# Zero fills of two large gradients: from an SBUF tile, or copied from DRAM to DRAM in 16 KB pieces

## The chip, the cores and the metric

The kernel runs on one core of a Trainium2 chip; the core that shares its memory is idle. The metric is the device time of one execution in microseconds (us). A ratio is the mean time of one kernel's fast runs over the mean of the other's fast runs of the same rounds, so it is not quite the ratio of the medians that are quoted.

## The reference, cut to what matters

The reference is the forward and backward pass of one decoding token through a modulated layer norm, a sliding-window attention over cached keys and values, and a gated MLP (FFN). For the change only the gradients of the caches matter:

```python
Hq, Hkv, Sk, Dh = (32, 4, 65536, 128)
W = min(4096, max(256, Sk // 4))                       # window: the last 4096 rows
k = jnp.repeat(k_cache[:, :, Sk - W:, :], rep, axis=1)
v = jnp.repeat(v_cache[:, :, Sk - W:, :], rep, axis=1)
...
_out, _vjp = jax.vjp(_f, A_x, A_k_cache, A_v_cache, A_wq, A_wo, B_w_gate, ...)
```

Outputs 2 and 3 are the gradients of the two caches, 4 x 65536 x 128 in bf16 each. Only the last 4096 rows of each head are not zero. The other 61440 rows are 15 MiB of zeros per head, and 8 heads in the two tensors make 120 MiB (125.8 MB) of zeros to write.

## The kernel before: the parts that matter

The zeros are written in 120 fills of 1 MiB from one zeroed tile. They are spread over the program by lists of counts (`Z_MOD`, `Z_FFN` and so on), so that they fill whatever time the other transfers leave. In the FFN loop ScalarE's queue issues them; elsewhere GpSimd's queue does.

```python
ZW = 4096
zeros = vt([P, ZW], "zeros", BF16)                     # 128 partitions x 8 KB
nc.vector.memset(zeros.bitcast(U32), 0)
...
for og in (out_2, out_3):
    for g in range(G):
        region = og[0, g, 0:SKW, :].rearrange("r d -> (r d)").rearrange("(p x) -> p x", p=P)
        for i in range(region.shape[1] // ZW):
            zregions.append(region[:, i * ZW:(i + 1) * ZW])
zleft = list(zregions)

def zero(n, after=None, q=None):
    for _ in range(n):
        if not zleft:
            return
        ins = (q or nc.gpsimd).dma_start(out=zleft.pop(0), in_=zeros[:, :])
        if after is not None:
            dep(ins, after)                            # wait for a step of the program: pacing
```

One round of the FFN loop (seven in all), cut to its transfers:

```python
zero(Z_FFN[5 * n], None, nc.scalar)
...
nc.sync.dma_start(out=wd_dram(out_8, n), in_=wd_t[n])
if n + 1 < NB:
    load_wg(n + 1)                                     # GpSimd queue, as load_wu
for j in range(KD):
    ...                                                # VectorE reads wu, ScalarE overwrites it
    if j % 4 == 3:
        zero(Z_FFN[5 * n + 1 + j // 4], None, nc.scalar)
nc.gpsimd.dma_start(out=dwu_view[:, :, n * FB:(n + 1) * FB], in_=wu)
...                                                    # the same for wg, two more places for fills
nc.gpsimd.dma_start(out=dwg_view[:, :, n * FB:(n + 1) * FB], in_=wg)
if n + 2 < NB:
    load_wu(n + 2)                                     # into a buffer that a store must leave first
```

## Time and profile before

| | before |
|---|---|
| time, median of 3 | 653.28 us (651.76 to 654.0) |
| bytes moved by the DMA engines | 262.63 MB, 404 GB/s on average |
| of these zero fills | 125.8 MB, 120 issues |
| memory traffic | 76.55 MB read, 185.60 MB written |
| busiest compute engine | VectorE, 49% of the span |

The row of DMA shares, the queues, the issues and the waits are shown in the prediction.

### The profile page before, as it was taken

Reading aid. Unit: us, or ns where it says so; the run is one execution under the profiler, and the core shown is the slowest. Engines: PE = TensorE matmul, PEld = TensorE weight load, DVE = VectorE, ACT = ScalarE, POOL = GpSimd, SP = SyncE. Lnnn points to the kernel's source line nnn. Section 1 sums busy time; section 2 is a strip of 40 time slices with the busy share of each in tenths; the row PEclk is TensorE's granted clock in tenths of the full one; section 3 lists DMA queues with packets and bytes.
Section 4 is the critical chain, followed back from the end, with each engine's and each line's share of the span. In section 5 each row is a group of like instructions: output and inputs, shape, how many; then the busy total and the mean of one; then the engine's idle time right before and its main releaser. Section 6 shows DMA issues by size and latency. Waiting matters only on the chain.

```text
span 650.8 us, 7106 instructions
## 1 busy us (share of the span) xinstructions
PE 149.7 (23%) x2784; PEld 127.4 (20%) x2784; DVE 319.7 (49%) x626; ACT 206.9 (32%) x306; POOL 83.0 (13%) x137
## 2 busy tenths in 40 slices
PE   3123227572201020010101101310670000424300
PEld 2123215572201020010101101300450000313200
DVE  3442005602737246081460814899700089996293
ACT  2000016611521613243133432789570000424800
POOL 2000000131010200102011010212111012112220
PEclk9999999865555555555555555575765555555555
DMA  8999999999999999999999999999999999999996
GB/s 335 430 428 422 426 426 413 404 418 397 421 425 415 416 417 393 414 388 408 417 356 419 361 409 415 392 382 412 388 415 422 415 425 426 425 407 388 410 411 251
DMA packets 43810, 262.63 MB, mean 404 GB/s; under 512 B 4096, under 2 KB 4096, under 8 KB 18432
## 3 DMA queue, kind: packets, MB, share of 16 engines
q0 software_dynamic: 23184, 131.08, 49.8%
q1 hardware_dynamic: 12048, 69.22, 26.0%
q10 hardware_dynamic: 8544, 61.88, 23.6%
q8 instruction: 22, 0.36, 0.2%
q14 instruction: 12, 0.10, 0.0%
HBM read 76.55 MB, written 185.60 MB: 403 GB/s over the span
## 4 chain that ended last, share of the span: by engine, by line
DMA 64%; DVE 14%; ACT 11%; PE 6%; issue 4%; POOL 0%; SPq 0%; POOLq 0%; ACTq 0%; DVEq 0%
DMA out_dram<-arena 28%; DMA arena<-in_B_w_gate_dram 18%; DMA arena<-in_w_mod_dram 7%; DVE arena L168 6%; DMA arena<-in_A_wq_dram 6%; ACT arena L172 5%; DMA arena<-in_A_k_cache_dram 5%; DVE junk L168 3%; PE tp_kv L342 2%; DVE arena L164 1%; ACT arena L345 1%; PE gu_ps L476 1%; ACT arena L230 1%; ACT du_b L508 1%; DMA out_dram<-dx_orow 1%
## 5 line engine op out<-in xcount | busy, mean ns | idle before, releaser
L168 DVE CUSTOM_DVE_ANT_0 arena<-arena 128x4096 bf16<-128x4096 bf16 (+1 forms) x24 | 80.1, 3350 | 51.4 <-DMA arena<-in_w_mod_dram 51.4
L476 PE MATMUL gu_ps<-h_bf,arena 128*128 128x1 bf16 x448 | 16.9, 172 | 192.1 <-DMA arena<-in_B_w_up_dram 103.5
L151 DVE TENSOR_TENSOR hh<-sg,gu_ps 128x4 f32<-128x4 f32 x7 | 1.1, 158 | 119.4 <-ACT om L481 119.4
L136 POOL DMA_DIRECT2D out_dram<-zeros x61 | 33.6, 554 | 185.0 <-PE q_ps L311 49.8
L476 PEld LDWEIGHTS <-arena 128*128 128x128 bf16 x448 | 16.2, 118 | 193.9 <-issue 166.7
L172 ACT ACTIVATE arena<-du_b,h 128x512 bf16<-128x512 bf16 x56 | 35.3, 710 | 36.0 <-DMA arena<-in_B_w_down_dram 32.3
L649 PEld LDWEIGHTS <-arena 8*128 8x128 bf16 x256 | 24.9, 127 | 106.1 <-issue 102.7
L172 ACT ACTIVATE arena<-dg_b,h 128x512 bf16<-128x512 bf16 x56 | 35.3, 708 | 26.4 <-issue 14.4
L345 ACT COPY arena<-tp_kv 128x1024 bf16<-128x1024 bf16 x13 | 13.1, 1010 | 89.7 <-PE tp_kv L342 89.7
L653 ACT CAST arena<-ps_kv 128x512 bf16<-128x512 f32 x32 | 16.1, 691 | 77.2 <-DMA out_dram<-arena 77.2
L168 DVE CUSTOM_DVE_ANT_0 junk<-arena,b1k 128x1024 bf16<-128x1024 bf16 x28 | 34.2, 1222 | 8.6 <-DMA arena<-in_B_w_down_dram 8.1
L168 DVE CUSTOM_DVE_ANT_0 arena<-arena,b1k 128x1024 bf16<-128x1024 bf16 x32 | 36.7, 1221 | 0.4 <-ACT b1k L230 0.4
L168 DVE CUSTOM_DVE_ANT_0 arena<-arena,du_b 128x512 bf16<-128x512 bf16 x56 | 34.8, 686 | 3.5 <-ACT du_b L508 3.5
L168 DVE CUSTOM_DVE_ANT_0 arena<-arena,dg_b 128x512 bf16<-128x512 bf16 x56 | 34.8, 685 | 0.0
L172 ACT ACTIVATE arena<-b1k,o_col 128x1024 bf16<-128x1024 bf16 x32 | 33.4, 1142 | 0.0
L649 PE MATMUL ps_kv<-DO_hd,arena 8*128 8x128 bf16 x128 | 15.3, 280 | 77.9 <-ACT arena L653 77.2
L342 PE MATMUL tp_kv<-ident_bf,arena 128*128 128x128 bf16 x256 | 22.1, 252 | 20.7 <-DMA arena<-in_A_k_cache_dram 13.0
L160 DVE COPY arena<-tp_kv 128x1024 bf16<-128x1024 bf16 x19 | 13.0, 690 | 28.1 <-PE tp_kv L342 28.1
L480 ACT ACTIVATE sg<-gu_ps 128x4 f32<-128x4 f32 x7 | 1.2, 174 | 76.3 <-PE gu_ps L476 76.3
L342 PEld LDWEIGHTS <-arena 128*128 128x128 bf16 x256 | 19.2, 115 | 23.6 <-DMA arena<-in_A_k_cache_dram 13.9
L429 POOL DMA_DIRECT2D arena<-in_B_w_up_dram x7 | 6.2, 890 | 134.4 <-DMA out_dram<-arena 134.4
L655 ACT ACTIVATE arena<-ps_kv 128x512 bf16<-128x512 f32 x32 | 16.1, 624 | 21.8 <-DMA out_dram<-arena 21.8
(185 smaller groups left out, 377.3 us busy)
## 6 DMA issues: line engine op xcount, KB each, us to landing
out_dram<-zeros POOLq DMA_DIRECT2D x61, 1024.0 KB, 20.4
out_dram<-zeros ACTq DMA_DIRECT2D x59, 1024.0 KB, 20.9
out_dram<-arena POOLq DMA_DIRECT2D x46, 1024.0 KB, 20.8
arena<-in_A_wq_dram SPq DMA_DIRECT2D x16, 1024.0 KB, 21.1
arena<-in_w_mod_dram SPq DMA_DIRECT2D x8, 1536.0 KB, 29.9
arena<-in_A_wo_dram SPq DMA_DIRECT2D x8, 1024.0 KB, 22.2
arena<-in_w_mod_dram SPq DMA_DIRECT2D x8, 1024.0 KB, 23.9
arena<-in_B_w_down_dram SPq DMA_DIRECT2D x7, 1024.0 KB, 11.9
```

Source lines behind the costliest of these rows:

```text
L136: ins = (q or nc.gpsimd).dma_start(out=zleft.pop(0), in_=zeros[:, :])
L160: return nc.vector.tensor_copy(out=out, in_=a)
L164: return nc.vector.tensor_scalar(out=out, in0=a, scalar1=s1, scalar2=None, op0=op0)
L168: return nc.vector.tensor_tensor_reduce(out=out, in0=w, in1=b, scale=1.0, scalar=0.0, op0=ALU.mult, op1=ALU.add, accum_out=acc)
L172: return nc.scalar.activation(out=out, in_=b, func=ACT.Copy, scale=col)
L230: last = nc.scalar.copy(out=o, in_=ps[:, :])
L342: nc.tensor.transpose(tp[:, t8 * P:(t8 + 1) * P], src[:, g, t_ * DH:(t_ + 1) * DH], ident_bf[:, :])
L345: last = nc.scalar.copy(out=o, in_=tp[:, :])
L476: nc.tensor.matmul(gu[:, half * 4 + jj:half * 4 + jj + 1], lhsT=w[:, j, jj::4], rhs=h2_bf[:, j:j + 1], start=(j == 0), stop=(j == KD - 1))
L649: nc.tensor.matmul(ps[:, t4 * DH:(t4 + 1) * DH], lhsT=rows[32 * g:32 * g + HG, t_ * P:(t_ + 1) * P], rhs=hd[32 * g:32 * g + HG, :], start= ...
L653: nc.scalar.copy(out=o, in_=ps[:, :])
L655: nc.scalar.activation(out=o, in_=ps[:, :], func=ACT.Copy, scale=float(scale))
```

## The change

The intent is larger pieces for the engines, without room for them in SBUF: one fill writes a first megabyte from the tile, and the other 119 copy that megabyte from DRAM to DRAM as 64 rows of 16 KB.

```diff
-            region = og[0, g, 0:SKW, :].rearrange("r d -> (r d)").rearrange("(p x) -> p x", p=P)
-            for i in range(region.shape[1] // ZW):
-                zregions.append(region[:, i * ZW:(i + 1) * ZW])
+            region = og[0, g, 0:SKW, :].rearrange("r d -> (r d)").rearrange("(i q x) -> i q x", q=64, x=8192)
+            for i in range(region.shape[0]):
+                zregions.append(region[i])
 ...
+    zsrc = zleft.pop(0)
+    first = nc.gpsimd.dma_start(out=zsrc.rearrange("a b -> (a b)").rearrange("(p x) -> p x", p=P), in_=zeros[:, :])
+
     def zero(n, after=None, q=None):
 ...
-            ins = (q or nc.gpsimd).dma_start(out=zleft.pop(0), in_=zeros[:, :])
+            ins = (q or nc.gpsimd).dma_start(out=zleft.pop(0), in_=zsrc, max_dma_last_dim=16384)
+            dep(ins, first)
```

So three things change at once: where a fill reads, how long its packets are, and how its rows lie in the output (a contiguous megabyte instead of 128 runs of 8 KB at a distance of 120 KB).

## The prediction

> **What bounds the kernel now.** I read the page's slices first, because they say whether any resource is full from end to end.
>
> ```profile
> DMA  8999999999999999999999999999999999999996
> GB/s 335 430 428 422 426 426 413 404 418 397 421 425 415 416 417 393 414 388 408 417 356 419 361 409 415 392 382 412 388 415 422 415 425 426 425 407 388 410 411 251
> DMA packets 43810, 262.63 MB, mean 404 GB/s; under 512 B 4096, under 2 KB 4096, under 8 KB 18432
> ```
>
> Every slice but the first and the last has the 16 DMA engines at least 90% busy. No compute engine comes near: VectorE, the busiest, has 49% of the span. So the kernel is 262.63 MB divided by the rate of the DMA engines, and a change helps or hurts by what it does to engine time per byte, or by opening holes in the DMA row. The rate is about 426 GB/s in the good slices and 360 to 415 in the others.
>
> Next the queues, then the issues, to see who the bytes belong to.
>
> ```profile
> q0 software_dynamic: 23184, 131.08, 49.8%
> q1 hardware_dynamic: 12048, 69.22, 26.0%
> q10 hardware_dynamic: 8544, 61.88, 23.6%
> ...
> HBM read 76.55 MB, written 185.60 MB: 403 GB/s over the span
> ```
>
> ```profile
> out_dram<-zeros POOLq DMA_DIRECT2D x61, 1024.0 KB, 20.4
> out_dram<-zeros ACTq DMA_DIRECT2D x59, 1024.0 KB, 20.9
> out_dram<-arena POOLq DMA_DIRECT2D x46, 1024.0 KB, 20.8
> ```
>
> The shares of the three data queues add to 99.4%: packets stand end to end on the engines. The zero fills are 120 issues of 1 MiB, 125.8 MB or 48% of all bytes; 61 go through the GpSimd queue (q0), 59 through the ScalarE queue (q10, which moves almost nothing else).
>
> The trace's packet records give the unit costs. A 2048-byte packet takes 84 ns, a 4096-byte one 159, an 8192-byte one 309 and a 12288-byte one 460 (medians on the queues where they are least disturbed). That is a line: about 151 ns per 4096 bytes (27.1 GB/s) plus some 7 to 8 ns per packet. Loads into SBUF and stores out of it have the same 309 ns. Against these floors the means are higher: 316 ns for q0's 8192-byte packets (10880), 324 for q10's (7552), 169 against 159 for the 10240 of 4096 bytes. Summed over all data packets and divided by 16 engines, these stalls are about 22 us of the span; the fills on q10 have (324.3 - 309) x 7552 / 16 = 7.2 us of it.
>
> Last the waits (who waited for what: us in total, times, longest) and the shares of the chain that ended last, to see what a delayed transfer would do.
>
> ```profile
> POOL arena L429 <- DMA out_dram<-arena: 134.4, 5, 30.2
> ...
> PE gu_ps L476 <- DMA arena<-in_B_w_up_dram: 103.5, 4, 28.0
> ```
>
> ```profile
> DMA 64%; DVE 14%; ACT 11%; PE 6%; issue 4%; POOL 0%; SPq 0%; POOLq 0%; ACTq 0%; DVEq 0%
> ```
>
> In the FFN stage (about 138 to 412 us) the loop is paced by the GpSimd queue: a store must land before the next weight load goes into its buffer, and TensorE waits for that load. Fills share the engines with these packets. Between 262 and 284 us the records show about 55 packets of 4096 bytes from q0 and 48 of 8192 from q10 in each 1.5 us: near one for one, so fills take two thirds of the bytes while both queues hold work.
>
> **What the Trainium skill says.** "DMA: Bandwidth & Descriptors", section "Queues, rings and completion order", says each engine serves its queues in turn, a packet at a time; the one-for-one counts agree. The same page, section "Why small descriptors are slow (HBM only)", gives a fixed overhead of about 3 cycles a packet inside the engine. The trace agrees in kind: 7 to 8 ns is that and a little more. "Advanced Engine Details and Errata", section "DMA Bandwidth Details", puts an engine at 27.2 GB/s and each SBUF port at the same 27.2. The slope of 27.1 fits, but cannot say which of the two limits, since every transfer of the kernel before that I can attribute to a tensor touches SBUF. "HBM Reference", section "Specifications (TRN2)", gives about 716 GB/s for the memory that a pair of cores shares. The trace reaches 403 on average, so it does not test that.
>
> **The change, part by part.** Compute order and the number of fills stay. The first fill is still written from the zero tile; the other 119 read that megabyte back from DRAM, as 64 rows of 16 KB instead of 128 of 8 KB. The instruction lists are otherwise the same; GpSimd gets one wait, for the first fill to land, and the rotation of its completion semaphores moves by one place.
>
> Packets: 119 x 64 = 7616 of 16 KB replace 15232 of 8 KB. On the line above a 16 KB packet costs 4 x 151 + 7.5 = 611 ns against 2 x 309 = 618. Saved: 7616 x 7 ns / 16 = 3.3 us.
>
> Stalls: a fill no longer reads SBUF, and it issues half as many packets. I take half of the 7.2 us found on q10 as gone: -3.6 us. This is a choice; part of those stalls arises when 1 KB rows of the FFN gradients are stored at the same time, and those stay.
>
> HBM: the new reads are 119 x 1.0486 = 124.8 MB. Total HBM traffic goes from 262.1 to 387 MB, or about 595 GB/s over an unchanged time. That is below the page's 716 but no longer far, and fills are not spread evenly. Fills alone at the engine rate of 427 GB/s would need 854. In the FFN a 16 KB fill packet now alternates with a 4 KB packet, so fills take 16/20 of the bytes and the demand is 427 x 1.8 = 769. At a ceiling of 716 the engines would move 716 / 1.8 = 398 GB/s in such stretches. The 59 fills there are 61.9 MB, with their companions 77.3 MB: 77.3 MB at 398 instead of 427 is 194 - 181 = 13 us. Outside the FFN many fills run beside loads or stores at a lower share. I take half of the 13, since requests spread by the queues and the ceiling may not be felt so sharply: +6 us (estimate from the page's figure and the trace's rates).
>
> Order on the engines: in the FFN the weight loads and stores of q0 go from a third of the bytes to a fifth while fills are waiting, from about 142 to 85 GB/s. The fills are finite, about 8 to 10 MB per round of some 40 us, so they finish sooner and the rest then has the engines alone. Total work stays; it costs only if the DMA row shows holes while compute catches up. ScalarE still holds fills back by its place in the program, which limits this in both directions. I set it to 0 with a risk of +1 to +4 us in each of seven rounds.
>
> The new wait: the five initial fills were issued at 3.3 us; now four follow only after the first lands, some 10 us later. SyncE's 20 MB of loads fill the engines then. 0 us.
>
> Sum: 653.3 - 3.3 - 3.6 + 6 + 0 + 0 = 652 us.
>
> **The rivals.** First, HBM becomes the bound. Reads and writes of the same memory, in lockstep at megabyte distances, may reach well below 716. At 550 GB/s overall, 387 MB takes 704 us; at 600, 646 us. Against it: the kernel before stores and loads together at 425 GB/s with packets at their floor. For it: stretches with mixed small stores already show packets 10 to 25% over the floor.
>
> Second, a DRAM to DRAM packet costs the engine much more than 611 ns, because the read's and the write's delays do not overlap. Nothing in the trace shows such a data packet. At 900 ns, the 7616 packets add 7616 x 289 / 16 = 138 us: about 790. I give this one in ten.
>
> Third, the SBUF port and not the engine is the 27 GB/s limit, and DRAM copies run faster. At 31 GB/s a packet would take 529 ns, and 7616 x 82 / 16 = 39 us go: about 610, if HBM allows it. Against it: the 17 packets of 8192 bytes on the instruction queue q14, which load no tensor, have the same median of 309 ns. One in ten.
>
> Fourth, the larger fill packets starve the FFN's loads and open DMA holes: up to 7 x 4 = 28 us, about 680.
>
> **Range and chances.** The engine-limited case lies between 640 (all stalls of fills gone, no HBM cost) and 660. HBM and the order of packets can only push upwards, and are more likely than a faster engine. So the range goes further up than down: 632 to 705. Faster by over 2% (below 640) needs the third rival, or nearly every fill stall gone: 0.2. Within 2%: 0.45. Slower: 0.35.
>
> **What would show it.** Right: 16384-byte packets on q0 and q10 near 611 ns, HBM traffic near 387 MB, the DMA row still at nines, and mean 8192-byte packets of others no slower. HBM as the bound: 16 KB packets well over 611 ns mainly where fills are dense, and loads and stores beside them slowed too. A costly packet: over 611 ns even where other traffic is thin, and the others unchanged. A faster engine: packets under 600 ns. Starved loads: DMA slices below nine in the FFN with longer waits of TensorE on weight loads. The prediction is wrong in its centre if the median 16 KB packet is below 590 or over 680 ns.

## More of the kernel before

To see later where time goes, the span is cut at three events: the start of the transposes that wait for the last of the four loads of keys, the first product of the FFN loop (with the up weights), and the end of the FFN loop. This view gives, for each stretch in us from the start, its length, the busy time (and instructions) of each engine, TensorE's clock, the share in which the DMA engines were busy, and what they moved:

```profile
0.00:96.80 96.80, 24.77 (x677) 22.51 (x677) 25.43 (x41) 6.08 (x8) 8.14 (x21) 1.00 0.99 411
96.80:160.60 63.80, 37.76 (x696) 33.25 (x697) 22.45 (x52) 23.45 (x29) 10.67 (x18) 0.75 1.03 410
160.60:414.20 253.60, 30.83 (x728) 27.97 (x727) 120.88 (x352) 86.49 (x137) 21.83 (x25) 0.50 1.01 404
414.20:650.80 236.60, 56.34 (x683) 43.71 (x683) 150.94 (x183) 90.94 (x133) 42.40 (x73) 0.54 0.98 398
```

The last two numbers of each line are what to read. The DMA engines are full in every stage (a share above 1 comes from packets that overlap a little in the records), and they move 398 to 411 GB/s throughout.

## The result, and the profile after

The changed kernel takes 689.54 us (686.18 to 690.53, 4 runs) against 653.5 us of the kernel before in the same rounds. The ratio is 1.0547 with a 95% interval of 1.0506 to 1.0589: slower.

The slices, the queues and the memory traffic of the changed kernel, the answer to the first lines in the prediction:

```profile
DMA  8999999999999899899999999999999999999996
GB/s 343 429 428 427 419 422 408 397 333 370 367 372 372 310 371 377 304 370 348 375 357 395 347 346 343 385 390 396 368 423 423 404 408 428 425 426 411 395 423 247
...
q0 software_dynamic: 19344, 131.08, 48.8%
q1 hardware_dynamic: 12048, 69.22, 25.6%
q10 hardware_dynamic: 4768, 61.88, 23.6%
...
HBM read 201.33 MB, written 185.60 MB: 563 GB/s over the span
```

A slice is 17.2 us here. The first eight, up to about 137 us, are about as fast as before (397 GB/s in the eighth, 404 before), with fills from DRAM running in them. From the ninth to the twenty-ninth the rate falls to 304 to 396 GB/s, and it recovers with the thirtieth. Two of those slow slices are also below nine tenths busy. So there are two losses: engines that are busy but move less, and engines with nothing to do. The reads grew by 124.8 MB as worked out.

The same cut by events, in the changed kernel:

```profile
0.00:99.90 99.90, 24.75 (x677) 22.54 (x677) 25.44 (x41) 6.08 (x8) 8.26 (x22) 1.00 0.99 411
99.90:175.30 75.40, 37.67 (x696) 33.08 (x697) 22.31 (x52) 23.42 (x29) 10.70 (x19) 0.71 1.01 382
175.30:451.40 276.10, 30.70 (x728) 27.92 (x727) 121.08 (x352) 86.12 (x137) 21.34 (x24) 0.50 0.97 359
451.40:687.30 235.90, 56.20 (x683) 43.54 (x683) 151.08 (x183) 91.22 (x133) 42.75 (x72) 0.54 0.98 397
```

Of the 36.5 us, 22.5 are in the FFN loop (276.1 against 253.6), 11.6 in the attention stage before it and 3.1 at the start; the backward stage after it is even 0.7 shorter. (The cuts are at steps of the program, so the stages do not move the same bytes: the attention stage moves 2.6 MB more than before, the loop 3.5 MB less.) Most of the 3.1 us is the sixth fill at the start: it is 1.05 MB, at 411 GB/s an estimated 2.6 us, which the end has less to move. In the FFN the rate went from 404 to 359 GB/s, and the DMA share from 1.01 to 0.97.

The packet records tell the busy part (q0 is the GpSimd queue, q1 SyncE's, q10 ScalarE's). The floor of a packet is its bytes at 27.12 GB/s plus 7 ns, which reproduces the 309 ns of 8 KB. The 16 KB packet has its median at 611 ns on q0, precisely the predicted floor, and 614 on q10, but its means are 655 and 685 ns. The 4 KB packets of the FFN rose from 168 to 190 ns in the mean within the FFN loop. Summed over all data packets and divided by 16 engines, the time over the floor went from 23.1 to 53.2 us, which is +30.1. The packets that were saved give -3.3. The mean engine's idle time (span less busy) went from 2.2 to 11.7 us, +9.5. Together that is +36.3 of the 36.5 us. Because packets overlap in the records, the idle times are too small by a few us; their differences are what counts.

Two waits of the kernel before that the prediction does not show (us in total, times, longest), then the waits, the issues with their median time to landing, and the engines' shares of the chain that ended last in the changed kernel (its L434 and L437 are L429 and L432 of the kernel before):

```profile
PE gu_ps L476 <- DMA arena<-in_B_w_gate_dram: 64.6, 7, 25.2
...
POOL arena L432 <- DMA out_dram<-arena: 28.0, 4, 8.5
```

```profile
POOL arena L434 <- DMA out_dram<-arena: 134.3, 5, 34.1
PE gu_ps L481 <- DMA arena<-in_B_w_gate_dram: 110.7, 6, 36.4
PE gu_ps L481 <- DMA arena<-in_B_w_up_dram: 103.2, 5, 28.1
...
POOL arena L437 <- DMA out_dram<-arena: 75.6, 4, 37.0
```

```profile
arena<-in_B_w_gate_dram POOLq DMA_DIRECT2D x7, 1024.0 KB, 14.7
```

```profile
out_dram<-out_dram POOLq DMA_DIRECT2D x60, 1024.0 KB, 20.7
out_dram<-out_dram ACTq DMA_DIRECT2D x59, 1024.0 KB, 16.8
...
arena<-in_B_w_gate_dram POOLq DMA_DIRECT2D x7, 1024.0 KB, 19.9
```

```profile
DMA 71%; DVE 15%; ACT 5%; PE 5%; issue 3%; SPq 0%; POOL 0%; ACTq 0%; POOLq 0%; DVEq 0%
```

The single issue line is the gate load of the kernel before, the three after it are of the changed kernel. TensorE's wait for gate weights grew from 64.6 to 110.7 us, GpSimd's wait before it may load them from 28.0 to 75.6. A gate load lands 19.9 us after its issue where it took 14.7, while ScalarE's fills land in 16.8 instead of 20.9 us: so fills seem to have got ahead of the loads that the loop waits for. These waits do not measure the loss: in a run below with long packets but no reads, TensorE waits 102.5 us for gate weights, and the whole kernel takes only 0.5% longer. The chain that ended last has 71% DMA where it had 64%.

### The profile page after: what moved, and what is told of

It reads as the page before. It is cut to its first block, busy times and chain, and to the rows that moved or that the text cites. A ratio compares the mean times of both kernels' runs of the same rounds, so it can differ in the third digit from the quotient of the medians.

```text
span 687.3 us, 7106 instructions
## 1 busy us (share of the span) xinstructions
PE 149.3 (22%) x2784; PEld 127.1 (18%) x2784; DVE 319.9 (47%) x626; ACT 206.8 (30%) x306; POOL 83.0 (12%) x137
## 2 busy tenths in 40 slices
DMA packets 36194, 262.63 MB, mean 382 GB/s; under 512 B 4096, under 2 KB 4096, under 8 KB 18432
## 4 chain that ended last, share of the span: by engine, by line
DMA 71%; DVE 15%; ACT 5%; PE 5%; issue 3%; SPq 0%; POOL 0%; ACTq 0%; POOLq 0%; DVEq 0%
DMA out_dram<-arena 24%; DMA arena<-in_B_w_gate_dram 15%; DVE arena L173 8%; DMA arena<-in_A_wo_dram 7%; DMA arena<-in_w_mod_dram 7%; DMA out_dram<-out_dram 6%; DMA arena<-in_A_wq_dram 6%; DMA arena<-in_A_k_cache_dram 5%; DVE junk L173 2%; DVE arena L169 1%; PE gu_ps L481 1%; PE tp_kv L347 1%; ACT du_b L513 1%; ACT arena L350 1%; DMA out_dram<-dx_orow 1%
## 5 line engine op out<-in xcount | busy, mean ns | idle before, releaser
L481 PE MATMUL gu_ps<-h_bf,arena 128*128 128x1 bf16 x448 | 16.7, 172 | 214.8 <-DMA arena<-in_B_w_gate_dram 110.7
L140 POOL DMA_DIRECT2D out_dram<-out_dram x60 | 31.1, 521 | 177.9 <-PE q_ps L316 54.1
L177 ACT ACTIVATE arena<-dg_b,h 128x512 bf16<-128x512 bf16 x56 | 35.3, 707 | 25.5 <-DMA out_dram<-out_dram 9.4
L347 PEld LDWEIGHTS <-arena 128*128 128x128 bf16 x256 | 19.1, 114 | 23.4 <-DMA arena<-in_A_k_cache_dram 13.7
L434 POOL DMA_DIRECT2D arena<-in_B_w_up_dram x7 | 6.2, 893 | 134.4 <-DMA out_dram<-arena 134.3
## 6 DMA issues: line engine op xcount, KB each, us to landing
out_dram<-out_dram ACTq DMA_DIRECT2D x59, 1024.0 KB, 16.8
```

The source lines that it names most:

```text
L140: ins = (q or nc.gpsimd).dma_start(out=zleft.pop(0), in_=zsrc, max_dma_last_dim=16384)
L177: return nc.scalar.activation(out=out, in_=b, func=ACT.Copy, scale=col)
L347: nc.tensor.transpose(tp[:, t8 * P:(t8 + 1) * P], src[:, g, t_ * DH:(t_ + 1) * DH], ident_bf[:, :])
L481: nc.tensor.matmul(gu[:, half * 4 + jj:half * 4 + jj + 1], lhsT=w[:, j, jj::4], rhs=h2_bf[:, j:j + 1], start=(j == 0), stop=(j == KD - 1))
```

## The experiments

Two theories stood at first. **Memory ceiling**: reads and writes share the memory's bandwidth, and a copy asks twice. **Order**: engines serve queues packet by packet, so longer fill packets take a larger share and the FFN's own transfers wait. Twelve kernels were run.

### The fills alone

The body of the changed kernel is replaced by its fills, in turn on two queues. All other outputs stay unwritten, so the result is wrong.

```diff
+    for i in range(len(zleft)):
+        zero(1, None, nc.gpsimd if i % 2 else nc.scalar)
+    return
```

The 716 GB/s in the next text is the figure of "HBM Reference" that the prediction cites; twice the 356 GB/s that the text takes from the trace is 712.

> The changed kernel's fills alone, nothing else (all other outputs left unwritten, so wrong on purpose): one fill of 1 MiB from SBUF, then 119 DRAM to DRAM in 16 KB pieces from the first megabyte, in turn on the ScalarE and the GpSimd queue. Memory-ceiling theory (reads plus writes share about 716 GB/s, as 2 us stretches of fills alone in the changed kernel's trace suggest: 356 GB/s copied): 124.8 MB at some 356 GB/s is 350 us, plus some 12 us for start and first fill, about 360 us, with the mean 16 KB packet near 730 ns although its median beside loads was 611. Order theory (the large packets only starve others, the copy itself is at the engine's 27 GB/s): 124.8 MB at 427 GB/s is 292 us, about 305 in all, packets at 611 ns.

Measured: 406.2 us, longer than both theories said. The second kernel does the same with the fills of the kernel before:

> The same 120 fills alone from the SBUF tile in 8 KB pieces, as in the kernel before (wrong on purpose). Both theories: 125.8 MB at 427 GB/s, 295 us plus some 10, about 305 us, 8 KB packets at 309 ns. If it takes longer, writes alone have a limit of their own.

Measured: 315.15 us. In the third, each fill reads another megabyte:

```diff
-            ins = ...dma_start(out=zleft.pop(0), in_=zsrc, max_dma_last_dim=16384)
+            ins = ...dma_start(out=zleft.pop(0), in_=zcache.pop(0), max_dma_last_dim=16384)
```

> As the fills alone from DRAM, but each of the 119 reads its own megabyte of the key and value caches, not the same one 119 times (wrong on purpose, values of the caches land in the outputs). Memory-ceiling theory: the same time as with the one megabyte, within 3%. Hot-spot theory (119 reads of one megabyte crowd the same banks): clearly faster than with the one megabyte, towards 305 us.

Measured: 402.83 us, 0.8% less than with the one megabyte (one run each), so the repeated source is not the cause. And in 8 KB pieces:

```diff
-  rearrange("(i q x) -> i q x", q=64, x=8192)      ... max_dma_last_dim=16384
+  rearrange("(i q x) -> i q x", q=128, x=4096)     ... max_dma_last_dim=8192
```

> The fills alone from DRAM, in 8 KB instead of 16 KB pieces (wrong on purpose, other outputs unwritten). Addresses are the same: each engine still gets 64 KB of each megabyte. Memory-ceiling theory: the copy is held by the memory, not by the engine's packets, so the time is that of 16 KB pieces, 406 us within 3%. If small pieces themselves are gentler to the memory, under 380 us.

Measured: 403.76 us. The length of the pieces does not matter to the copy alone. The middle of the run with 16 KB pieces, and of the run from SBUF, in the view by stretches (no TensorE here; the end of the line is clock, DMA share, GB/s):

```profile
20.00:380.00 360.00, 0.00 (x0) 24.91 (x50) 1.00 1.00 317
```

```profile
20.00:300.00 280.00, 0.00 (x0) 26.65 (x51) 1.00 1.01 415
```

Both have the engines full for the whole stretch. From DRAM they move 317 GB/s, which is 634 GB/s at the memory; from SBUF 415. The engines are busy, but with packets held up: the 16 KB packets have a 25th percentile at the floor of 611 ns and means of 792 and 859 ns on the two queues. So there is a limit for copies that the engines' own rate does not explain, at about 635 to 645 GB/s of reads plus writes (2 x 317 to 2 x 322 over the three kernels). All of them write the same addresses in the same order, so whether the limit depends on where the rows lie was not tested.

### Copies mixed with stores

If this is a ceiling on total traffic, its effect must follow from the share of copies alone. Three kernels put 59 copies from DRAM on one queue and 60 MiB of fills from SBUF on the other, with piece sizes meant to set the share: 8 KB against 8 KB, 8 KB against 4 KB, and 16 KB against 4 KB as in the FFN of the changed kernel. Their outputs are wrong, which doesn't matter for the times.

```diff
+    for i in range(59):
+        zero(1, None, nc.scalar)                       # copy from DRAM
+        for _ in range(per):
+            nc.gpsimd.dma_start(out=small.pop(0), in_=zeros[:, 0:2048])   # 0:4096 in the first
```

> Fills alone again (wrong on purpose), half and half: 59 DRAM to DRAM fills in 8 KB pieces on the ScalarE queue beside 60 MB of fills from SBUF in 8 KB pieces on the GpSimd queue. Served packet by packet, half of the bytes are copies from DRAM, so 427 GB/s of engine rate asks 1.5 x 427 = 640 GB/s of the memory. Memory-ceiling theory with the 638 GB/s that the fills alone reached (2 x 319): just fits, about 410 to 420 GB/s moved, about 312 us. If the copies from DRAM are slow by themselves, whatever runs beside them, their mean packet stays near the 391 to 425 ns that it had alone and the time is near 360 us.

> As the half and half mix, but the SBUF fills are in 4 KB pieces, like the FFN's own packets beside 8 KB pieces: two thirds of the bytes are copies while both queues work. Ceiling at 638: 638 / 1.67 = 382 GB/s until the copies are done (243 us), then SBUF fills alone at about 405: about 335 us in all.

> The FFN's mix in the changed kernel: 16 KB copies from DRAM on the ScalarE queue beside SBUF fills in 4 KB pieces on the GpSimd queue, four fifths of the bytes copies. Ceiling at 638: 638 / 1.8 = 354 GB/s until the copies are done (219 us), then about 405: about 349 us in all, and while both run the 4 KB packets are slowed as well (well over 159 ns).

Measured: 305.98, 335.57 and 347.44 us, where 312, 335 and 349 were expected. The stretches with both queues at work, in the order of the three kernels:

```profile
20.00:280.00 260.00, 0.00 (x0) 26.47 (x50) 1.00 1.01 427
```

```profile
20.00:220.00 200.00, 0.00 (x0) 26.12 (x49) 1.00 1.02 382
260.00:320.00 60.00, 0.00 (x0) 23.97 (x45) 1.00 1.02 402
```

```profile
20.00:220.00 200.00, 0.00 (x0) 15.94 (x30) 1.00 1.01 362
260.00:320.00 60.00, 0.00 (x0) 23.24 (x44) 1.00 1.02 393
```

At half copies nothing is lost: 427 GB/s moved, 1.5 x 427 = 640 at the memory, and the copies' mean packet is 310 ns. At two thirds (67% of the bytes in the packet records of this stretch) it is 382 and 1.67 x 382 = 638; at a planned four fifths, 78% in the records, it is 362 and 1.78 x 362 = 644. Copies are not slow in themselves; beside stores, all traffic together stops near 640 to 645 GB/s. The last lines hold a caution: 4 KB fills from SBUF, which run alone in those stretches, move 393 to 402 GB/s and not the 412 that 159 ns per 4096 bytes would give, so a little of the loss in these two kernels is the small stores' own. In the second kernel they stand 9.4 us over their floor beside copies (25.5 MB) and 2.6 us alone (24.1 MB).

### Piece size in the whole kernel

The changed kernel with 8 KB pieces has the same addresses and the same memory traffic, and fill packets as long as before (the same edit as for the fills alone):

> The changed kernel with its DRAM to DRAM fills in 8 KB pieces (128 rows), so that a fill packet is as long as in the kernel before and only the source and the place of the rows differ. Memory-ceiling theory: the loss stays, 685 to 695 us, since 387 MB are moved either way. Order theory (16 KB packets crowd out the FFN's weight loads and stores): most of the loss goes, 655 to 665 us, and the slices below nine in the FFN's DMA row fill up.

Measured: 666.08 us, ratio 1.0216 (1.0181 to 1.0251). Both theories missed. Ceiling alone would have kept the loss; most of it went, as order said, yet 2.2% stayed (slower beyond doubt, but the interval leaves open whether by 2%), and the FFN loop moves 394 GB/s where it moved 404. Doubling the packet costs another 23 us that neither part explains alone.

> The changed kernel with its fills in 4 KB pieces. Packets: 30464 of 159 ns instead of 15232 of 309 in the kernel before, 30464 x 159 - 15232 x 309 = 137 us over 16 engines, +8.6 us. Order and memory together: fills now take half of the FFN's bytes and ask 640 GB/s, so hardly any stall is added there; what remains is the stretches with fills alone, about half of the 12 us that 8 KB pieces lost. About 668 us, and 4 KB stores near their 169 ns of before. If piece size helps for its own sake and not by share, below 660.

```diff
-  rearrange("(i q x) -> i q x", q=64, x=8192)      ... max_dma_last_dim=16384
+  rearrange("(i q x) -> i q x", q=256, x=2048)     ... max_dma_last_dim=4096
```

Measured: 673.6 us, ratio 1.0325 (1.0289 to 1.0361), 5.6 us more than expected. The 4 KB packets on q0, copies among them, keep their mean (168 ns), but the copies on q10 have 177 ns over a floor of 159. So a share of one half did not free them of stalls in the full kernel, as it did in the mix with 8 KB stores. Why small copies are held up there stays open.

### Which fills lose

```diff
+            if q is None:                              # second kernel: q is not None
                 ins = (q or nc.gpsimd).dma_start(out=zleft.pop(0), in_=zsrc, max_dma_last_dim=16384)
                 dep(ins, first)
+            else:                                      # the same megabyte from the tile, 8 KB pieces
+                ins = (q or nc.gpsimd).dma_start(out=..., in_=zeros[:, :])
```

> The changed kernel with only the 59 fills of the ScalarE queue (the FFN stage) taken from the SBUF tile again (8 KB pieces); the 60 of the GpSimd queue stay DRAM to DRAM in 16 KB. Order and memory theories together: the loss sits where DRAM fills run beside the FFN's small packets, so most of the 36 us goes: 655 to 665 us. If the loss came evenly from all fills, about 671 us.

> The reverse: only the 59 FFN fills are DRAM to DRAM in 16 KB pieces, the 60 others come from SBUF. Order and memory theories together: nearly the whole loss stays, 675 to 690 us. Even loss: about 671 us.

Measured: 666.29 us (ratio 1.0214, interval 1.0159 to 1.0268, again unclear at the 2% mark) with the FFN's fills from SBUF, 682.35 us (1.0443, 1.0399 to 1.0488) with only the FFN's fills from DRAM. The two losses, 12.4 and 28.4 us, add to somewhat more than the 36 us of the change. The traces place them: with the FFN's fills back in SBUF, the FFN loop moves 399 GB/s, nearly as before, and its start is at 177.0 instead of 160.6 us, so the GpSimd queue's fills lose their time before it. There, between 130 and 175 us in the changed kernel, the mean 16 KB packet takes 679 ns; between 20 and 130 us, beside loads, 614. With only the FFN's fills from DRAM, the loop starts at 163.7 and moves 364 GB/s in 278.4 us.

```profile
177.00:425.00 248.00, 30.64 (x728) 27.85 (x727) 120.88 (x352) 86.52 (x137) 21.32 (x24) 0.50 1.00 399
```

### Long packets without reads

To have 16 KB packets without extra reads, the FFN's 59 fills come from a resident block of SBUF that is 16 KB wide (its content is not zero, so these outputs are wrong). The other fills come from the tile. All write contiguous megabytes, as in the changed kernel, so this also tests the new place of the rows.

```diff
+            if q is not None:
+                ins = q.dma_start(out=zleft.pop(0), in_=arena[0:P:2, int(G_OFF * KIB):int((G_OFF + 16) * KIB)])
```

> The 59 FFN fills in 16 KB pieces but out of SBUF (64 alternate partitions of the resident 16 KB weight block, so the outputs there are wrong on purpose), the other 60 as before from the zero tile: 16 KB packets without any added memory reads. Pure order theory (long packets crowd out the FFN's 4 KB packets): the loss of the FFN is there without DRAM sources, 670 to 685 us, with slices under nine in the DMA row. Pure memory theory: 645 to 655 us. If both are needed, something between, 655 to 668.

Measured: 656.71 us, ratio 1.0054 (1.0025 to 1.0084). Pure order falls. With long packets alone the FFN loop moves 396 GB/s instead of 404, and the idle time of the mean engine over the run is 7.2 us where it was 2.2. The new place of the rows can hardly cost more than the 0.5% that the whole kernel lost and the 1.7 us that its longer packets save (3776 x 7 ns / 16).

The FFN loop in four corners, each line from its own kernel: SBUF in 16 KB pieces, DRAM in 8 KB (the whole changed kernel in 8 KB), DRAM in 16 KB in the FFN alone:

```profile
164.50:420.60 256.10, 30.83 (x728) 27.96 (x727) 121.18 (x352) 86.57 (x137) 21.52 (x24) 0.50 0.99 396
```

```profile
170.50:424.20 253.70, 30.65 (x728) 27.86 (x727) 120.80 (x352) 86.41 (x137) 21.30 (x24) 0.50 1.01 394
```

```profile
163.70:442.10 278.40, 30.79 (x728) 27.91 (x727) 120.83 (x352) 86.32 (x137) 21.46 (x24) 0.50 0.98 364
```

The packet records, added up for the loop (us of the mean engine, except where a unit is given):

| fills of the FFN | length of the loop | MB moved | GB/s | over the floor | idle |
|---|---|---|---|---|---|
| SBUF, 8 KB (before) | 253.6 | 102.5 | 404 | 11.2 | -1.7 |
| SBUF, 16 KB | 256.1 | 101.4 | 396 | 12.7 | 3.4 |
| DRAM, 8 KB | 253.7 | 99.9 | 394 | 18.6 | -2.7 |
| DRAM, 16 KB (all fills) | 276.1 | 99.0 | 359 | 34.6 | 7.4 |
| DRAM, 16 KB (FFN only) | 278.4 | 101.2 | 364 | 34.6 | 4.2 |

The loops do not move the same bytes, so their lengths alone mislead; the last two columns do not have this fault. (Idle times below zero come from packets that overlap in the records.) Against the kernel before, long packets alone add 1.5 us over the floor and 5.1 us of idle time. DRAM sources alone add 7.4 us over the floor and no idle time. Both together add 23.4 us over the floor and 9.1 us of idle time, far more than the sum. With 8 KB pieces a fill takes two thirds of the bytes while it shares an engine with 4 KB packets, and the mix asks for 1.67 x 427 = 713 GB/s of the memory. With 16 KB pieces it takes about four fifths and asks 769. The mixes give what is then moved, 382 and 362 GB/s; the loops moved 394 and 359. From 8 KB to 16 KB copies the loop gained 16.0 us over the floor (7.6 in ScalarE's fills, 5.0 in the 4 KB packets, 3.4 in SyncE's loads) and 10.1 us of idle time. So the two causes need each other; what in the memory holds the packets up was not found.

## Why the prediction was right or wrong

The measured 689.54 us lie inside the stated range of 632 to 705, and the first rival is what happened, with the fourth beside it; the signs named for these two are the ones that appeared. The range held because the first rival at 550 GB/s (704 us) set its upper end, and the run moved 563. The centre of 652 and the odds, which put "within 2%" first, were wrong.

**Packets.** Right. The 16 KB packet has its median at the predicted 611 ns, and the -3.3 us is in the balance. That the line's 7 to 8 ns a packet are the three cycles of the skill page "and a little more" is not shown: the prediction turned no cycles into time, and no run here has the length of one.

**Rivals two and three.** Both fall by the same number. A copy costs the engine no more than a load or store of the same length (medians of 309 ns for 8 KB copies and loads, 611 for 16 KB copies and for 16 KB stores out of SBUF), and the SBUF port does not seem to be what holds a packet to 27 GB/s, since a packet that touches no SBUF has the same floor.

**Stalls, -3.6 us.** This term has the wrong sign. Reading DRAM instead of SBUF took no stall away. Time over the floor rose by 30.1 us, in the fills (27.7 us over the floor after, on both queues) and in the others: the 4 KB packets went from 7.0 to 13.6 us over it.

What the next term costs shows up in the records as time over the floor too, so the two are one loss seen from two sides.

**HBM, +6 us.** The mechanism was right and the size wrong; this is the term that was mis-sized most. It took the skill page's 716 GB/s as the ceiling, found 13 us and halved it. The runs show 634 to 645 for copies, alone and among stores. The four-fifths mix moves 362 GB/s and not 398, so the term's own sum becomes 77.3 MB at 362 instead of 427, which is 214 - 181 = 33 us, not 13 (22 us against the 404 GB/s that the loop before really moved). It also set the fills outside the FFN at nothing, and those of the GpSimd queue cost 12.4 us by themselves when only they read DRAM; the choice to halve had no support in the trace.

**Order, 0 us with a risk of 1 to 4 us a round.** The step said that finite fills only finish sooner. The risk was real: the mean engine's idle time rose by 9.5 us over the run, 9.1 of it in the FFN loop. Gate loads land later there (19.9 us after 14.7); that compute then starts with too little left to move is the likely reason, not a tested one. Long packets alone give only 5 us more of it; with copies that are also slower it is twice that.

**The new wait, 0 us.** Right within the profile's means: the first stretch runs at 411 GB/s in both kernels. But not four fills follow the first, as the text has it: the trace shows six issued together at 15.5 us, the five of the start and one of the next step. The kernel so has one fill more up front, most of the 3.1 us by which the first cut comes later, and gets it back at the end.

The test that the prediction set for its centre was a median packet between 590 and 680 ns. The median was 611 and the centre still failed: 65% of the 16 KB packets sat within 1% of the floor, and 24% took over 680 ns. It should have asked for the mean, and for the mean in the FFN (684 ns on q10).

## What to carry to other kernels

When a kernel is bound by its DMA engines, count the traffic at the memory too: a copy from DRAM to DRAM costs the engines one transfer and the memory two (here 124.8 MB more reads with the same 262.63 MB moved by the engines), and the dense stretches decide, not the average (563 GB/s over this span looked harmless). The length of a packet sets a queue's share where queues compete (beside 4 KB pieces, 78% of the bytes for 16 KB pieces and 67% for 8 KB), so longer pieces on background traffic are not free even when each byte gets cheaper, and here they hurt most where the background traffic was also near another limit. Judge packets by their mean against their floor, stage by stage; a median hides the queueing.

No version that beats both kernels came out. Where 16 KB copies run at their floor, as beside the loads of the first 130 us, they save 7 ns in 618; for the 29 fills issued before the FFN that is at most 29 x 64 x 7 ns / 16 = 0.8 us, less than the spread of the runs.

## What the Trainium skill lacked or had wrong

- "HBM Reference", section "Specifications (TRN2)", gives about 716 GB/s per domain. Copies from DRAM to DRAM alone reached 317 to 322 GB/s over 360 us, 634 to 644 at the memory; mixed with stores it was 638 to 644. Beside loads into SBUF, a stretch of 17 us in the changed kernel (20 to 37 us) had 430 GB/s moved and 666 at the memory, with the mean 16 KB packet still at 612 ns. So the reachable figure depends on the mix, and the page has none for it.
- "DMA: Bandwidth & Descriptors", section "Latency and other measured facts", has 214 GB/s per direction as the full rate of copies between HBM tensors, without saying whether they pass through SBUF. Direct copies moved 317 to 322 here, and an unobstructed 16 KB packet took 611 ns, which is 26.8 GB/s on each engine.
- The same page, section "Queues, rings and completion order", describes turns of a packet at a time, but not what this does to the shares of queues whose packets differ in length. With 16 KB against 4 KB pieces and both queues full, the copies were 78% of the bytes in the packet records; one for one would be 80%. With 8 KB against 4 KB they were 67%, as one for one gives.
